# A fused attention and two-layer MoE kernel: another fixed order for its first 36 positions

## The chip, the cores and the metric

The kernel runs on one core of a Trainium2 chip. The metric is the device time of one execution in microseconds (us). The kernel before took 653.89 us as the median of three runs (653.66 to 656.63).

Engine names as in the profile: PE is TensorE (matmuls; PEld its weight loads), DVE is VectorE, ACT is ScalarE, POOL is GpSimd, SP is SyncE, which issues nearly all DMAs here.

## The reference

Attention over batch 2, 8 heads, 768 positions, head dimension 64, in float32. Each query sees the 31 keys of a band around it, and 24 block keys: the maximum over each block of 32 keys, with log(32) added to its score; its value is the mean of the block's values. Softmax over both together, then two dense layers over the 1536 tokens:

```
k_sum = k.reshape(B, H, nb, block, D).max(axis=3)
v_sum = v.reshape(B, H, nb, block, D).mean(axis=3)
scores_s = scale * np.einsum('bhsd,bhnd->bhsn', q, k_sum) + np.log(block)
a = softmax([where(|i - j| < 16, scale * q k^T, -1e9), scores_s])
x = a @ [v, v_sum]                       # 1536 tokens x 512
y = ((x @ w_a) * (x @ w_b)) @ w_out      # d_ff 1536
h = y @ w_in;  g = h - np.tanh(h)        # d_ff 2048
out = g @ w_out2
```

## The kernel before

Attention is cut into 24 units of 64 queries (12 of each batch element). A unit is a chain: transposed queries times a window of 96 keys and the 24 block keys on PE (`T2m`), mask and row minimum on DVE (`tt`), exponential and row sum on ACT (`ex`), one over the sum on DVE (`rb`), the normalization of the 128x480 scores (`nm`), transposes on PE (`T3t`), the copy out of PSUM (`T3e`), the product with the values on PE (`T4m`), and the split of the result into a high and a low half (`T4h` on ACT, `T4l` on DVE).

The dense layers work in blocks of 512 tokens, so block 0 needs units 0 to 7. Every float32 matmul is three matmuls of split operands: high by high, high by low, low by high. A weight tile arrives as raw words and is decoded: two ACT passes (`da`, `db`), a clamp (`dc`, line 179), a shift (`dd`, line 767), a bit mix (`de`, line 769) and an add (`df`, line 771), the last three mostly on DVE; then it is split by ACT (`sh`, line 776) and a subtraction (`sl`, line 779). The finished add frees the staging buffer for a later weight load.

A "position" is one weight tile times one block: 12 matmuls of 128x512. Positions 0 to 35 are block 0 of the first layer: `x @ w_a` (kind a), `x @ w_b` (kind b) and the product with `w_out` (kind o), in the order a0 b0 a1 b1 o0 a2 b2 o1 ... a11 b11 o10 o11. Their matmuls are `Mp<position>_<quarter>` (lines 802 for a and b, 796 for o). Between b and o the two results are multiplied (`Mt`, DVE, line 808) and split (`Mh`, ACT, line 811; `Ml`, DVE, line 813).

What sets the order: up to position 35 everything (attention units 0 to 15, the decoding of the weights, the 36 positions) is issued by `op` in the sequence of one string, `SEQ`, of 838 names; each engine executes its instructions in that order and waits at each for what it needs. A table, `EC`, says for each name which engine does it (`A` ACT, `D` DVE, `P` POOL). Attention units 0 to 15 are in this string; their PE operations stand between quarters of positions. From position 36 on, the scheduler of the framework orders all engines but SP. A few of its instructions are placed into the end of the fixed part: the decoding of the next layer's weights (lines 154, 155 on ACT, 161, 164, 165 on DVE, tiles `x21a` and `x21b`) and single matmuls of line 350.

`FILL` names operations in front of which `warm` (line 582) issues transposes of the identity, whose results are not used. `warm` is called for the operations `T1t`, `T2m`, `T3t` and `T4m` only.

Of the kernel before, what the change touches and what calls it, by code (L numbers as in the profile page):

```python
# [39 lines left out]
def band_attention_moe_kernel(ctx: ExitStack, tc: tile.TileContext, q, k, v, w_a, w_b, w_out, w_in, w_out2, out):  # L40
# [3 lines left out]
    B, H, S, D = q.shape  # L44
# [18 lines left out]
    def st(shape, tag, bufs=1, dt=F32):  # L63
        return sb.tile(shape, dt, tag=tag, bufs=bufs, name=tag)
# [510 lines left out]

    qbs = [qbd, qbd2, qbd3, qbd4]
    P_A, P_B = ([j for j in range(HEAD_P) if pos[j][0] is fn] for fn in (pos_a, pos_b))
    FILL = {'T1t4': 6}

    def warm(n, d):  # L580
        for _ in range(FILL.get(n, 0)):
            nc.tensor.transpose(d, ident, ident)

    def op(n):
        import re
        k, a = re.match("([A-Za-z]+[0-9](?:t|ea|eb|e|m|h|l)|[A-Za-z]+)(.*)", n).groups()
        i, _, c = a.partition("_")
        i, c = int(i or 0), int(c or 0)
        e = EC.get(n, "A")
        if k == "LK":  # L590
# [79 lines left out]
        elif k == "tt":  # L670
# [3 lines left out]
            e = st([128, NP, NK], ("e", "ta", "tg", "w")[i // 2] if i < 8 else "e", 36 if i in (6, 7) else 2)  # L674
# [11 lines left out]
        elif k == "ex":  # L686
            e, nm, sm = at_x[i]
# [4 lines left out]
        elif k == "rb":  # L692
            e, nm, sm = at_x[i]
            nc.vector.tensor_scalar(sm, sm, 1e-9, None, op0=ALU.add)
            nc.vector.reciprocal(sm, sm)
        elif k == "nm":
            eng = e if i > 7 else "P"
            e, nm, sm = at_x[i]
            if eng == "A":
                for p in range(NP):  # L700
# [4 lines left out]
        elif k == "T3t":  # L705
            e = at_x.pop(i)
# [54 lines left out]
        elif k in ("dc", "dd", "de", "df"):  # L761
# [117 lines left out]
```

## Time and profile before

| | |
|---|---|
| three runs | 653.66, 653.89, 656.63 us |
| profiled execution | 653.74 us; its span 652.0 us, 1.7 us lie around the span |
| PE busy | 633.5 us (97% of the span) |
| DVE, ACT, POOL busy | 499.3, 475.4, 206.6 us |
| granted TensorE clock | 0.996 on average |

A span is the time from the first to the last instruction. The page cuts it in 40 slices of 16.3 us; PE is at 7 tenths in the first slice and over 9 tenths from the fourth to the last but one. Busy PE time counts the full latency of overlapping matmuls, so how fast PE works is read from the start of one matmul to that of the next: a row "2.88 us x12" followed by a row that starts 2.72 us later means 0.227 us for each.

### The profile page before, as it was taken

The numbers are of one execution on the slowest core, as the hardware profiler recorded it, in microseconds if no ns is written. First come the engines' busy times: TensorE is split into PE (matmuls) and PEld (weight loads), VectorE is DVE, ScalarE is ACT, GpSimd is POOL, SyncE is SP. The second block draws the span as 40 slices with busy tenths as digits, with TensorE's granted clock in tenths as the row PEclk, the third lists the DMA queues.
The fourth block names the chain that finished last, engine by engine and source line by source line (L and its number), as shares of the span: only waits on it lengthen the run. The fifth ranks groups of instructions, "written<-read, shape, count | busy, mean of one in ns | idle before, by whom it ended". The sixth has DMA issues, their size and how long they took to land.

```text
span 652.0 us, 9585 instructions
## 1 busy us (share of the span) xinstructions
PE 633.5 (97%) x3238; PEld 517.6 (79%) x3238; DVE 499.3 (77%) x1007; ACT 475.4 (73%) x1001; POOL 206.6 (32%) x218
## 2 busy tenths in 40 slices
PE   7779999999999999999999999999999999999997
PEld 5667887878788878788888888888888888888885
DVE  5999999988764767747877758877777877777775
ACT  4889899987576797636655548777777777777774
POOL 6852232211100110001111144544444544444441
PEclk9999999999899999999999999999999999999999
DMA  9989995644503435414434100000010000100001
GB/s 203 256 229 250 262 268 174 185 126 116 162 17 118 145 110 158 145 51 147 157 133 156 37 1 1 1 0 2 1 65 1 1 1 0 40 26 2 2 0 65
DMA packets 81677, 62.11 MB, mean 95 GB/s; under 512 B 45716, under 2 KB 72340, under 8 KB 81628
## 3 DMA queue, kind: packets, MB, share of 16 engines
q1 hardware_dynamic: 79276, 60.32, 33.0%
q0 software_dynamic: 2352, 1.18, 1.5%
q8 instruction: 25, 0.41, 0.3%
q14 instruction: 24, 0.20, 0.1%
HBM read 54.00 MB, written 7.34 MB: 94 GB/s over the span
## 4 chain that ended last, share of the span: by engine, by line
PE 75%; DVE 9%; DMA 7%; ACT 5%; issue 2%; SPq 1%; POOL 0%; DVEq 0%; ACTq 0%; POOLq 0%
PE acc L439 20%; PE pb L350 12%; PE pa L350 12%; PE acc L378 8%; PE pt L350 5%; PE ps L350 5%; DMA stage<-in_moe_w_in_dram 4%; PE pb L802 3%; PE acc L796 3%; PE pa L802 2%; DVE w L769 1%; ACT e L283 1%; DVE w L771 1%; DMA x21a<-in_moe_w_out_dram 1%; DMA x20a<-in_q_dram 1%
## 5 line engine op out<-in xcount | busy, mean ns | idle before, releaser
L185 POOL TENSOR_TENSOR wsp<-w,wsp 128x512 fp32r<-128x512 f32 x97 | 127.7, 1335 | 139.8 <-ACT wsp L184 139.8
L184 ACT ACTIVATE wsp<-w 128x512 fp32r<-128x512 f32 x165 | 99.1, 621 | 14.2 <-PE acc L378 8.8
L179 POOL TENSOR_SCALAR w<-w 128x512 f32<-128x512 f32 x46 | 34.9, 764 | 174.6 <-ACT w L154 81.5
L439 PE MATMUL acc<-wsp,gh 128*128 128x512 f32 x256 | 78.8, 389 | 0.0
L185 DVE TENSOR_TENSOR wsp<-w,wsp 128x512 fp32r<-128x512 f32 x68 | 48.4, 712 | 31.7 <-ACT wsp L184 31.5
L378 PE MATMUL acc<-gh,wsp 128*128 128x512 f32 x192 | 64.2, 394 | 0.0
L350 PE MATMUL pa<-XB,wsp 128*128 128x512 f32 x240 | 60.5, 395 | 0.0
L350 PE MATMUL pb<-XB,wsp 128*128 128x512 f32 x240 | 59.6, 393 | 0.3 <-DVE tg L808 0.3
L343 ACT ACTIVATE gh<-tg 128x512 fp32r<-128x512 f32 x56 | 34.9, 623 | 29.9 <-DVE tg L366 29.6
L439 PEld LDWEIGHTS acc<-wsp,gh 128*128 128x128 f32 x256 | 48.0, 188 | 10.0
L350 PEld LDWEIGHTS pb<-XB,wsp 128*128 128x128 f32 x240 | 44.5, 188 | 9.8 <-issue 0.7
L350 PEld LDWEIGHTS pa<-XB,wsp 128*128 128x128 f32 x240 | 44.3, 188 | 9.0
L439 PE MATMUL acc<-wsp,gl 128*128 128x512 f32 x128 | 49.8, 389 | 0.0
L439 PE MATMUL acc<-wsp,vw 128*128 128x512 f32 x192 | 46.5, 390 | 0.0
L350 PE MATMUL pa<-XA,wsp 128*128 128x512 f32 x192 | 46.1, 389 | 0.0
L350 PE MATMUL pb<-XA,wsp 128*128 128x512 f32 x192 | 46.1, 389 | 0.0
L344 DVE TENSOR_TENSOR gl<-tg,gh 128x512 fp32r<-128x512 f32 x56 | 38.5, 688 | 9.7 <-ACT gh L343 9.4
L439 PEld LDWEIGHTS acc<-wsp,vw 128*128 128x128 f32 x192 | 35.9, 188 | 8.2 <-ACT vw L343 0.4
L350 PEld LDWEIGHTS pb<-XA,wsp 128*128 128x128 f32 x192 | 36.0, 188 | 7.5
L350 PEld LDWEIGHTS pa<-XA,wsp 128*128 128x128 f32 x192 | 36.0, 188 | 7.5
L378 PEld LDWEIGHTS acc<-gh,wsp 128*128 128x128 f32 x192 | 36.0, 188 | 7.5
L802 PE MATMUL pb<-XA,wsp 128*128 128x512 f32 x144 | 37.2, 398 | 1.2 <-DVE tg L808 1.1
(336 smaller groups left out, 1440.9 us busy)
## 6 DMA issues: line engine op xcount, KB each, us to landing
stage<-in_moe_w_out_dram SPq DMA_DIRECT2D x19, 512.0 KB, 3.5
stage<-in_moe_w_in_dram SPq DMA_DIRECT2D x16, 512.0 KB, 4.5
stage<-in_moe_w_a_dram SPq DMA_DIRECT2D x8, 512.0 KB, 4.3
w<-wsc SPq DMA_DIRECT2D x16, 256.0 KB, 3.5
vw<-in_v_dram SPq DMA_DIRECT2D x19, 192.0 KB, 5.0
stage<-in_moe_w_b_dram SPq DMA_DIRECT2D x7, 512.0 KB, 5.9
wsc<-x21a SPq DMA_DIRECT2D x8, 256.0 KB, 4.5
wsc<-x21b SPq DMA_DIRECT2D x8, 256.0 KB, 4.6
```

Source lines behind the costliest of these rows:

```text
L179: eng.tensor_scalar(rf, rf, HI_HI, HI_LO, op0=ALU.min, op1=ALU.max)
L184: nc.scalar.activation(s[:, 0, :], r, AF.Copy)
L185: eng.tensor_tensor(s[:, 1, :], r, s[:, 0, :].bitcast(F32), op=ALU.subtract)
L283: nc.scalar.activation(e[:, p, :], e[:, p, :], AF.Exp, scale=-1.0, bias=nm[:, p : p + 1], accum_out=sm[:, p : p + 1])
L343: nc.scalar.activation(dst[0], src, AF.Copy)
L344: eng.tensor_tensor(dst[1], src, dst[0].bitcast(F32), op=ALU.subtract)
L350: mm(dst, w, xx, start=(kk == 0 and n == 0), stop=(kk == KC - 1 and n == 2))
L378: mm(acc[blk][d][:, c0:c1], w, t, start=(f == 0 and c0 == 0 and n == 0), stop=(f == F1 - 1 and n == 2))
L439: mm(a[c], g[:, cs], s[:, i, :], start=(f == 0 and n == 0), stop=(f == F2 - 1 and n == 2))
L769: nc.vector.scalar_tensor_tensor(r, t[:, :, 1], -0x40000000, r, op0=ALU.bitwise_and, op1=ALU.bitwise_or)
L796: mm(acc[0][c], w, t, start=(f == 0 and m == 0), stop=(f == F1 - 1 and m == 2))
L802: mm(P_["M", i], w, t, start=(c == 0 and m == 0), stop=(c == KC - 1 and m == 2))
```

## The change

Three literals and one line change. `SEQ` keeps the same 838 names in another sequence. `EC` gets entries for `nm0` to `nm7`, and line 697, which sent the normalization of units 0 to 7 to POOL whatever the table said, now follows the table. Other entries of `EC` change too. `FILL` names `KP0` with 3 in place of `T1t4` with 6.

Engine choices that differ, before to after:

```
nm0 nm1 nm3 nm6 nm7    POOL -> DVE   (nm2 nm4 nm5 stay on POOL)
nm11 DVE -> ACT;  nm13 nm15 ACT -> DVE
T3e0 T3e1 T3e2 T3e3 T3e12  DVE -> ACT;  T3e7 ACT -> DVE
T1ea1 T1ea2 T1ea6  DVE -> ACT;  T1ea3 T1eb2  ACT -> DVE
W1 POOL -> DVE;  W4 DVE -> POOL;  W10 W11 ACT -> DVE;  V13 DVE -> ACT
dc0 dc1 dc2 dc7 dc12 dc16 dc22 dc23 dc28 dc30 dc33 dc35  POOL -> DVE
dc6 dc31 dc34  DVE -> POOL
sl1 POOL -> DVE;  df1 DVE -> POOL
vc2 POOL -> DVE;  vc3 vc7 DVE -> POOL;  vc4 ACT -> POOL
```

`W` and `V` copy the keys of a unit, `T1ea`/`T1eb` the transposed queries, `vc` the block values.

```diff
-    EC = {'T1ea0': 'A', 'T1eb0': 'A', 'T1ea1': 'D', ...
+    EC = {'T1ea0': 'A', 'T1eb0': 'A', 'T1ea1': 'A', ... 'nm0': 'D', 'T3e0': 'A', 'nm1': 'D', ...
...
-    FILL = {'T1t4': 6}
+    FILL = {'KP0': 3}
...
         elif k == "nm":
-            eng = e if i > 7 else "P"
+            eng = e
             e, nm, sm = at_x[i]
...
-    SEQ = '... Kt0 Ke0 Kt1 Kt3 Ke1 Kr0 Kt4 Kt2 ...
+    SEQ = '... Kt1 Kt0 Ke0 Kt2 Kt3 Kr1 Kr2 Ke1 ...
```

Which instruction now stands where, at three places. On POOL, the normalizations of the first units (line 703; 749 copies block values, 179 is a clamp). Lines with `-` are the kernel before:

```order
-L703 TENSOR_TENSOR e<-e,sm 128x480 x2
-L703 TENSOR_TENSOR ta<-ta,sm 128x480 x2
-L703 TENSOR_TENSOR w<-w,sm 128x480
+L703 TENSOR_TENSOR ta<-ta,sm 128x480
 L703 TENSOR_TENSOR tg<-tg,sm 128x480
 L749 TENSOR_SCALAR w<-w 24x512
-L749 TENSOR_SCALAR vw<-w 24x512 x2
-L179 TENSOR_SCALAR w<-w 128x512
-L703 TENSOR_TENSOR w<-w,sm 128x480
+L749 TENSOR_SCALAR vw<-w 24x512 x3
+L749 TENSOR_SCALAR w<-w 24x512
 L703 TENSOR_TENSOR tg<-tg,sm 128x480
```

Eight normalizations became three, and the clamp among them went away. On POOL right behind that, the clamps, the subtractions of the first weight tiles (779), the add of the second one (771) and the first accumulating load (223):

```order
 L703 TENSOR_TENSOR tg<-tg,sm 128x480
-L179 TENSOR_SCALAR w<-w 128x512 x2
-L779 TENSOR_TENSOR wsp<-w,wsp 128x512 x3
-L179 TENSOR_SCALAR w<-w 128x512
+L771 TENSOR_TENSOR w<-w,stage 128x512
+L779 TENSOR_TENSOR wsp<-w,wsp 128x512
 L223 DMA x20a<-in_v_dram 96x8x128
+L779 TENSOR_TENSOR wsp<-w,wsp 128x512
```

Three clamps and one subtraction left POOL for DVE, and one add came from DVE. On DVE, the end of the fixed part up to the last split `Ml11` (813); 808 is `Mt11`; 161, 164 and 165 belong to the next layer's weights. Before:

```order
L161 TENSOR_SCALAR x21a<-x21a 128x512
L771 ISA w<-stage,w 128x1024
L779 TENSOR_TENSOR wsp<-w,wsp 128x512 x2
L164 SCALAR_TENSOR_TENSOR x21a<-stage,x21a 128x512
L779 TENSOR_TENSOR wsp<-w,wsp 128x512
L161 TENSOR_SCALAR x21b<-x21b 128x512
L165 ISA x21a<-stage,x21a 128x1024
L808 TENSOR_TENSOR tg<-pb,ta 128x512
L164 SCALAR_TENSOR_TENSOR x21b<-stage,x21b 128x512
L779 TENSOR_TENSOR wsp<-w,wsp 128x512
L165 ISA x21b<-stage,x21b 128x1024
L813 TENSOR_TENSOR gl<-tg,gh 128x512
```

And the same stretch after:

```order
L779 TENSOR_TENSOR wsp<-w,wsp 128x512
L161 TENSOR_SCALAR x21b<-x21b 128x512
L779 TENSOR_TENSOR wsp<-w,wsp 128x512 x2
L164 SCALAR_TENSOR_TENSOR x21b<-stage,x21b 128x512
L161 TENSOR_SCALAR x21a<-x21a 128x512
L808 TENSOR_TENSOR tg<-pb,ta 128x512
L165 ISA x21b<-stage,x21b 128x1024
L164 SCALAR_TENSOR_TENSOR x21a<-stage,x21a 128x512
L779 TENSOR_TENSOR wsp<-w,wsp 128x512
L813 TENSOR_TENSOR gl<-tg,gh 128x512
L734 TENSOR_TENSOR XB<-pt,XB 128x4x64
L165 ISA x21a<-stage,x21a 128x1024
```

One of the six instructions of the next layer, an add of line 165, now stands behind the last split.

## Rows read from the trace of the kernel before

**Rows 1.** Busy us by engine (x instructions) in stretches, clock, DMA share, GB/s.

```profile
core 0: us, PE busy (x) PEld busy (x) DVE busy (x) ACT busy (x) POOL busy (x), PEclk, DMA share, GB/s
20.00:42.60 22.60, 15.02 (x195) 11.59 (x194) 22.09 (x73) 20.14 (x70) 16.51 (x17) 1.00 0.97 233
53.20:163.40 110.20, 110.11 (x637) 88.82 (x637) 102.24 (x248) 98.19 (x237) 25.76 (x31) 1.00 0.77 196
163.40:170.40 7.00, 5.38 (x15) 3.74 (x15) 3.63 (x7) 3.51 (x6) 0.61 (x1) 0.76 0.74 222
...
380.00:400.00 20.00, 20.00 (x90) 16.53 (x90) 13.06 (x21) 13.82 (x24) 8.24 (x7) 1.00 0.01 1
```

**Rows 2.** PE in order of time: start, us, instruction [idle before, releaser].

```profile
41.12 0.87 PE L582 MATMUL ps<-ident 128*128 128x128 f32 x6 [2.33 <-DVE XA L734]
41.83 0.60 PE L646 MATMUL ps<-ident,w 128*128 128x128 f32 x4
...
42.62 3.02 PE L802 MATMUL pa<-XA,wsp 128*128 128x512 f32 x12
...
53.17 3.02 PE L802 MATMUL pb<-XA,wsp 128*128 128x512 f32 x12 [1.11 <-DVE tg L808]
...
77.38 2.88 PE L802 MATMUL pa<-XA,wsp 128*128 128x512 f32 x12
...
157.47 2.88 PE L802 MATMUL pb<-XA,wsp 128*128 128x512 f32 x12
160.19 0.39 PE L796 MATMUL acc<-gh,wsp 128*128 128x512 f32 x1
...
164.97 0.51 PE L796 MATMUL acc<-gh,wsp 128*128 128x512 f32 x1 [0.67 <-ACT gh L811]
166.15 0.80 PE L796 MATMUL acc<-gl,wsp 128*128 128x512 f32 x1 [0.67 <-DVE gl L813]
...
170.35 0.60 PE L249 MATMUL pt<-ident,qn 128*128 128x128 f32 x4
```

**Rows 3.** DVE and POOL groups by shape, 0 to 171 us: busy us, mean ns | idle before.

```profile
L703 DVE TENSOR_TENSOR e<-e,sm 128x480 f32<-128x480 f32 x3 | 2.0, 652 | 0.0
L574 DVE COPY at<-acc 120x512 f32<-120x512 f32 x2 | 1.4, 686 | 0.0
L574 DVE COPY w<-kt 128x384 f32<-128x384 f32 x1 | 0.3, 345 | 0.0
L179 POOL TENSOR_SCALAR w<-w 128x512 f32<-128x512 f32 x30 | 23.6, 798 | 80.5 <-ACT w L758 64.9 <-DMA vw<-in_v_dram 11.6 <-PE ps L629 2.1
```

**Rows 4.** DVE in order of time.

```profile
26.67 0.42 DVE L574 COPY w<-w 24x512 f32<-24x512 f32 x1
27.02 1.21 DVE L574 COPY vw<-w 24x512 f32<-24x512 f32 x1
...
38.97 1.77 DVE L771 CUSTOM_DVE_ANT_0 w<-stage,w 128x1024 uint16<-128x1024 uint16 x1
...
41.65 0.41 DVE L734 TENSOR_TENSOR XA<-pa,XA 128x256 fp32r<-128x256 f32 x1
...
44.17 0.41 DVE L179 TENSOR_SCALAR w<-w 128x512 f32<-128x512 f32 x1
44.50 0.75 DVE L767 TENSOR_SCALAR w<-w 128x512 int32<-128x512 int32 x2
...
76.50 0.69 DVE L779 TENSOR_TENSOR wsp<-w,wsp 128x512 fp32r<-128x512 f32 x1 [1.05 <-ACT wsp L776]
...
164.20 0.68 DVE L779 TENSOR_TENSOR wsp<-w,wsp 128x512 fp32r<-128x512 f32 x1
164.81 0.68 DVE L165 CUSTOM_DVE_ANT_0 x21b<-stage,x21b 128x1024 uint16<-128x1024 uint16 x1
165.41 0.68 DVE L813 TENSOR_TENSOR gl<-tg,gh 128x512 fp32r<-128x512 f32 x1
```

**Rows 5.** POOL in order of time.

```profile
26.78 1.15 POOL L703 TENSOR_TENSOR w<-w,sm 128x480 f32<-128x480 f32 x1 [0.38 <-DVE sm L695]
...
38.65 1.53 POOL L779 TENSOR_TENSOR wsp<-w,wsp 128x512 fp32r<-128x512 f32 x1 [0.94 <-ACT wsp L776]
```

**Rows 6.** Who waited for whom on DVE, 0 to 171 us: total us, times, longest.

```profile
DVE wsp L779 <- ACT wsp L776: 2.7, 3, 1.1
DVE e L681 <- PE pt L268: 1.6, 2, 1.0
DVE XB L734 <- ACT XB L732: 1.5, 1, 1.5
DVE gl L813 <- ACT gh L811: 0.7, 1, 0.7
```

More of the change, by code (lines that the diff above doesn't have):

```diff
@@ new lines, in band_attention_moe_kernel @@
+    EC = {'T1ea0': 'A', 'T1eb0': 'A', 'T1ea1': 'A', 'T1eb1': 'A', 'T1ea2': 'A', 'T1eb2': 'D', 'T1ea3': 'D', 'T1eb3': 'D', 'W0': 'P', 'W1': 'D', 'W2': 'P', 'W3': 'P', 'W4': 'P', 'W5': 'P', 'W6': 'P', 'W7': 'P', 'nm0': 'D', 'T3e0': 'A', 'nm1': 'D', 'T3e1': 'A', 'nm2': 'P', 'T3e2': 'A', 'nm3': 'D', 'T3e3': 'A', 'nm4': 'P', 'T3e4': 'A', 'nm5': 'P', 'T3e5': 'A', 'nm6': 'D', 'T3e6': 'D', 'nm7': 'D', 'T3e7': 'D', 'vc0': 'D', 'vc1': 'D', 'vc2': 'D', 'vc3': 'P', 'vc4': 'P', 'vc5': 'P', 'vc6': 'P', 'vc7': 'P', 'dc0': 'D', 'df0': 'D', 'dc1': 'D', 'df1': 'P', 'dc2': 'D', 'df2': 'D', 'dc3': 'D', 'dc4': 'D', 'dc5': 'D', 'dc6': 'P', 'dc7': 'D', 'dc8': 'P', 'dc9': 'P', 'dc10': 'P', 'dc11': 'P', 'dc12': 'D', 'dc13': 'P', 'dc14': 'P', 'dc15': 'P', 'dc16': 'D', 'dc17': 'P', 'dc18': 'P', 'dc19': 'P', 'dc20': 'P', 'dc21': 'P', 'dc22': 'D', 'dc23': 'D', 'dc24': 'P', 'dc25': 'P', 'dc26': 'P', 'dc27': 'P', 'dc28': 'D', 'dc29': 'P', 'dc30': 'D', 'dc31': 'P', 'dc32': 'P', 'dc33': 'D', 'dc34': 'P', 'dc35': 'D', 'sl0': 'P', 'sl1': 'D', 'sl2': 'P', 'W8': 'D', 'W9': 'A', 'W10': 'D', 'W11': 'D', 'V12': 'A', 'W12': 'A', 'V13': 'A', 'W13': 'A', 'W14': 'A', 'W15': 'A', 'T1ea4': 'A', 'T1eb4': 'A', 'T1ea5': 'A', 'T1eb5': 'A', 'T1ea6': 'A', 'T1eb6': 'A', 'T1ea7': 'A', 'T1eb7': 'A', 'nm8': 'A', 'T3e8': 'A', 'nm9': 'A', 'T3e9': 'A', 'nm10': 'A', 'T3e10': 'A', 'nm11': 'A', 'T3e11': 'A', 'nm12': 'D', 'T3e12': 'A', 'nm13': 'D', 'T3e13': 'A', 'nm14': 'D', 'T3e14': 'A', 'nm15': 'D', 'T3e15': 'A', 'KE0': 'A', 'KE1': 'A', 'KE2': 'A', 'KE3': 'A', 'KE4': 'A', 'KE5': 'A'}
@@ new lines, in band_attention_moe_kernel @@
+    SEQ = 'LK0 LK1 LK2 LK3 LK4 LK5 Lq0 Lq1 Lq2 Lq3 Lv0 Lv1 Lv2 LV0 LV1 LV2 LV3 LV4 LV5 LV6 LV7 Lw0 Lw1 Lw2 Lw3 Lw4 Kt1 Kt0 Ke0 Kt2 Kt3 Kr1 Kr2 Ke1 W1 Ke2 W0 Kt4 W2 Kr4 Ke3 Kt5 Kr0 Kr3 T1t0 Kr5 W3 Ke4 T1eb0 Lq4 Ws1 T1ea0 T1t1 Ke5 Ws0 Ws2 T2m1 Ws3 T1t2 T2m0 W11 T1eb1 tt1 W5 W4 W10 T1ea1 T2m2 va0 T1t3 T2m3 tt0 T1ea2 T1eb2 W7 T2m5 ex1 T2m4 tt2 ex0 T1ea3 ex2 tt3 T1eb3 T2m7 W6 ex3 va1 va2 tt5 tt4 rb2 ex5 T2m6 tt7 ex7 vm nm2 tt6 vme T3t2 rb5 rb3 rb0 W8 rb1 nm0 T3t0 ex6 nm3 ex4 T3e0 Lk0 rb7 T3e2 da0 nm1 rb6 T3t3 T3t1 vc1 nm7 db0 T3t7 vc2 rb4 nm6 T3t6 T3e7 dc0 nm5 vc0 dd0 T3e3 da1 T3e6 T3t5 de0 dc1 T3e1 LA0 vc3 T4m2 da2 T4m0 vc7 db1 T4m7 vc6 df0 dd1 T4h2 dc2 T4h0 vc5 vc4 de1 dd2 T4l0 T4m3 T4h3 nm4 T4l2 T4m6 T4m1 df1 T4l3 T4h7 T4h1 T3t4 T4l1 T3e5 T4m5 T3e4 Lw5 sh0 T4m4 T4h5 T4h6 sl0 T4h4 T1t4 KP0 da4 T4l7 da3 T4l5 db2 T4l6 T4l4 Mp0_0 de2 dc4 T1ea4 LA1 Mp0_1 dc3 Mp0_2 sh1 T1eb4 df2 dd3 Lw6 Mp0_3 W9 dd4 T2m8 sl1 Mp1_0 de4 da5 de3 sh2 dc5 KR0 Lw7 Ma0 db3 tt8 dd5 Mp1_1 sl2 Mp1_2 db4 df3 da6 Mp1_3 Mp2_0 dc6 KE0 Lq5 sh3 Mt0 db5 df4 LV8 Mp2_1 sl3 Lk1 Mp2_2 da7 dd6 Mp2_3 Lq6 de5 T1t5 Lw8 dc7 Mh0 sh4 Ma1 Mp3_0 db6 df5 sh5 Ml0 Mp3_1 sl4 db7 dd7 Mp3_2 de6 ex8 de7 df6 sl5 Lw9 Mp3_3 da8 Mp4_0 Mt1 dc8 T2m9 T1eb5 Mp4_1 Mp4_2 LV9 sh6 rb8 df7 Lw10 dd8 Mp4_3 Mp5_0 Lk2 T1ea5 KP1 Mp5_1 sl6 db8 sh7 da9 da10 de8 db9 Mp5_2 Lw11 Mp5_3 Mh1 dc9 KR1 tt9 dc10 Mp6_0 df8 Mp6_1 db10 Lw12 dd9 KE1 sl7 de9 Mp6_2 nm8 Mp6_3 sh8 Ma2 db11 da11 T2m10 Lk3 Ml1 sl8 T3t8 df9 sh9 Lw13 Lw14 Lk4 dd10 da12 Mp7_0 ex9 tt10 Mp7_1 Mp7_2 dc11 de10 dc12 Mp7_3 df10 Mp8_0 sl9 Mp8_1 da13 Mp8_2 rb9 Mt2 T3e8 dc13 Mp8_3 Lq7 dd11 sh10 dd12 Mh2 de11 db12 nm9 sl10 Mp9_0 Lq8 KP2 Lw15 LA2 Ma3 Ml2 df11 KE2 de12 da14 Mp9_1 db13 sh11 dc14 dd13 KR2 Mp9_2 Mp9_3 Mt3 db14 Mp10_0 db15 da15 T2m11 df12 T3t9 Lw16 Mp10_1 sl11 Mp10_2 de13 Mh3 Mp10_3 Mp11_0 Mp11_1 tt11 dd14 Ml3 Mp11_2 dc15 sh12 da16 sl12 df13 dc16 Mp11_3 dd15 db16 Mp12_0 Lk5 de14 ex11 sh13 df14 KP3 ex10 Mp12_1 Mp12_2 T3e9 LA3 sl13 sh14 KR3 de15 rb11 df15 Lw17 dd16 Mp12_3 Mp13_0 KE3 T4m8 sl14 Ma4 T4m9 W12 sh15 T4h8 de16 Lw18 rb10 Lq9 T4l8 da17 T4h9 db17 T4l9 Mp13_1 dc17 da18 dd17 Mp13_2 sl15 Mt4 Mp13_3 Mp14_0 KP4 nm10 Mh4 dc18 Mp14_1 Mp14_2 df16 Mp14_3 Mp15_0 Mp15_1 Lw19 KE4 de17 Ml4 LV10 df17 da19 Mp15_2 KR4 dc19 db19 sh16 LV11 dd18 sl16 sh17 db18 KP5 Ma5 KE5 sl17 Lw20 dd19 Lw21 da20 nm11 Mp15_3 da21 db20 de18 Mp16_0 dc20 KR5 df18 Lw22 sh18 Lw23 de19 Mt5 V13 Mp16_1 dd20 Mp16_2 df19 Mp16_3 sl18 Mh5 sh19 Mp17_0 T1t6 da22 Mp17_1 Lw24 LV12 Mp17_2 de20 dc21 Mp17_3 sl19 Ml5 dd21 T1eb6 df20 Mp18_0 T1ea6 db21 da23 Mp18_1 de21 Mp18_2 dc23 dc22 sh20 V12 Mp18_3 sl20 dd22 db22 df21 Ma6 de22 Mp19_0 Mp19_1 T3t10 Mt6 Lw25 db24 da24 Mp19_2 Mp19_3 Mp20_0 dc24 dd23 dd24 T3e10 df22 T2m12 W13 sh21 Mp20_1 Mp20_2 Mp20_3 Mh6 sl21 tt12 Lw26 da25 de23 dc25 sh22 W14 Mp21_0 db23 Mp21_1 dd25 ex12 Ml6 df23 sh23 de24 T3t11 Mp21_2 sl22 T2m13 Mp21_3 da26 Lw27 df24 db26 tt13 db25 de25 dc26 Ma7 Mp22_0 da27 Lw28 sh24 Mp22_1 sl23 Mp22_2 dc27 W15 da28 Mt7 dd26 Mp22_3 dd27 T3e11 de26 Mh7 Mp23_0 df25 sl24 Mp23_1 Lw29 T4m10 da29 db27 df26 Ml7 Mp23_2 Lw30 Mp23_3 T4h10 sh25 T4l10 Mp24_0 Mp24_1 dc28 de27 rb12 mv0 Mp24_2 ex13 dd28 sh26 df27 mv1 Ma8 db28 de28 da30 mvE rb13 Lw31 T1t7 sl25 dc30 nm12 dd30 Mp24_3 sl26 nm13 Mt8 Mp25_0 T1eb7 Lw32 T1ea7 da31 LM12 T3t12 T2m14 sh27 db31 T3e12 tt14 sl27 Mp25_1 dc29 dc31 LM13 df28 dd29 Mp25_2 Mh8 db29 T4m11 Mp25_3 T4h11 Mp26_0 LV13 T3t13 ex14 da32 T4l11 T2m15 de29 Mp26_1 Mp26_2 Mp26_3 T3e13 de30 df29 tt15 rb14 LV14 dd31 nm14 T4m12 Lw33 Mp27_0 db30 Ml8 ex15 T4h12 T4m13 T4h13 rb15 db32 T4l12 LM14 sh29 Mp27_1 nm15 T3t14 T4l13 Lw34 dc32 df30 sh28 de31 Mp27_2 dd32 T3e14 T3t15 sl28 sl29 T3e15 Mp27_3 da34 LV15 sh30 LV16 Lw35 T4m14 LV17 T4m15 T4h15 T4l15 dc34 da33 Ma9 de32 df31 T4h14 Mp28_0 Mp28_1 Mp28_2 da35 df32 db33 Mp28_3 Mt9 LV18 sh32 dc33 dc35 sh31 Mp29_0 Mp29_1 sl30 dd35 Mp29_2 Mp29_3 Lw36 Mh9 db35 dd33 Mp30_0 dd34 db34 sl31 de33 Mp30_1 Ml9 Mp30_2 de35 Mp30_3 Mp31_0 Ma10 de34 df34 Mp31_1 sl32 Mp31_2 Mp31_3 df33 Mt10 sh34 Mp32_0 sh33 Mp32_1 Mp32_2 df35 sl33 Mp32_3 Mh10 Ml10 Mp33_0 sh36 sh35 Mp33_1 Mp33_2 sl34 Mp33_3 Mp34_0 Mp34_1 Lw37 Ma11 sl36 Mp34_2 sh37 sl35 Mp34_3 Mt11 Lw38 sl37 Mh11 Ml11 Mp35_0 T4l14 Mp35_1 sh38 Mp35_2 sl38 XE1 Mp35_3 XE3 XE2 XE0'
```

2 lines of the change are left out of this document (removed).

## The prediction

> **What bounds the kernel now.** I read the stretches first [rows 1]. From 53 us on TensorE (PE) is busy all the time, 110.1 of 110.2 us, and behind the fixed part too, 20.0 of 20.0 us in a later stretch. So the time is that at which the fixed part's matmuls end, plus a rest that PE works through without a pause. That rest begins at 170.35 us, with the transpose behind the last matmul of position 35 [rows 2], and neither its matmuls nor their number change. The change can move only this point, the head's end.
>
> Then PE in order of time [rows 2]. The first matmul of position 0 starts at 42.62; before that PE waits (15.0 us busy of 22.6 in 20 to 42.6 [rows 1]) and VectorE (DVE) is the full engine, 22.1 of 22.6 us. From 42.62 PE has one pause of 1.11 us, at 52, for the product `Mt0` on DVE, until position 34 (`o10`) starts at 160.19. At the end, position 35 waits for the high and the low half of the last product, and starts its second matmul only at 166.15. The granted clock of that stretch is 0.76 [rows 1], so part of it ran at 1.2 in place of 2.4 GHz.
>
> What PE would need without pauses: 160.19 - 42.62 - 1.11 = 116.46 us up to `o10`; 24 matmuls for `o10` and `o11` at 0.227 us (12 in 160.19 - 157.47 = 2.72 [rows 2]) are 5.44; two single matmuls of line 350 between them are 0.45. Together 122.35 us. From 42.62 that gives 164.97. The head's end is at 170.35, so 5.4 us are lost: 1.1 at 52, 4.3 at the end, where the last DVE split, `Ml11`, ends at 165.41 + 0.68 = 166.09 [rows 4] behind a full DVE queue.
>
> **The change part by part.**
>
> *DVE's load.* Back to back, a two-operand DVE instruction of 128x512 takes 0.60 us from start to start (164.20, 164.81, 165.41), a clamp 0.34 (44.17 to 44.50) [rows 4]. Twelve clamps come and three go: 9 x 0.34 = 3.1. Five normalizations of the first units come, at 0.65 less an overlap of 0.08 [rows 3]: 2.9. Of the later ones two come and one goes: 0.6. Five copies `T3e` go and one comes: -4 x 0.60 = -2.4 (0.69 long [rows 3]). One query copy goes net, -0.6. `sl1` comes and `df1` goes, 0. Key windows `W10` and `W11` come, two copies each (0.35 [rows 3] and a shorter one): 0.8. Net one copy of block values goes, 0.35 from start to start (26.67 to 27.02 [rows 4]), with `V13`: -0.5. Sum: +3.9 us of DVE work before the last split.
>
> *POOL's load and what it costs DVE.* A POOL instruction beside a DVE one can stretch it. While `sl0` ran for 1.53 us [rows 5], the add `df1` took 1.77 on DVE [rows 4], 1.1 more than the same add beside nothing (0.68, line 165). While a normalization ran on POOL at 26.78 [rows 5], a copy of block values took 1.21, 0.8 more than the one before it (0.42) [rows 4]; over the eight normalizations I count between 0 and 0.8, 0.3 in the mean. The clamps on POOL, 0.80 us each [rows 3], stretch DVE in only six of 30 places, by 0.4, so 0.1 in the mean. Five normalizations, nine clamps and one subtraction leave POOL: 5 x 0.3 + 9 x 0.1 + 0.7 = 3.1 us less stretching (0.7 for `sl1`, between the 1.1 of `sl0` and none). `df1` comes to POOL, which no row shows there: as a two-operand instruction over 128x512 it is bounded by no stretching and by `sl0`'s 1.1, and I take 1.1, the nearest row. Net 2.0 saved. One add of the next layer, 0.60, moves behind the last split. DVE's path to the last split grows by 3.9 - 2.0 - 0.6 = 1.3 us, to 167.4, if DVE waits as much as before.
>
> The Trainium skill, in "SBUF — State Buffer", states that VectorE, in an instruction with two SBUF inputs, and GpSimd, when it reads SBUF, take turns at a shared port pair, whichever comes second being blocked for the whole instruction of the other. By that, `df1` on POOL speaks against this change: an estimate from that rule is the whole instruction, 1.5 us as for `sl0`, in place of 1.1, and the sum would be 0.4 us later. The trace agrees in direction for `sl0` (1.1 of 1.5 us), but most of the clamps block nothing.
>
> *DVE's waits.* In the head DVE waits 2.7 us for `sh` on ACT, 1.6 for PE, 1.5 for one `T4h` and 0.7 for `Mh9` [rows 6], 6.5 in all. Four of these waits, 3.5 us, lie after 136 us, where the old order has DVE well ahead of PE. Counting instructions times their durations, DVE in the new order is 3 to 5 us less ahead there, while ACT's load is about 1 us smaller. A DVE that comes later finds its inputs ready. I take these 3.5 us as gone (0 at one end, 6.5 at the other): `Ml11` ends at 163.9.
>
> *The start of position 0.* It is set by the last low half of units 0 to 7, on DVE at 41.65 [rows 4]. Of the +3.9 us some 1.8 lie before that (five normalizations, three clamps, the window copies, less four `T3e`, `df1` and a copy), and about 0.9 of stretching goes, so DVE comes 0.9 later. Against it: the six idle transposes at 41.12 go (0.71 us to the next row's start at 41.83, so 0.7 on the way to position 0), since `KP0` never reaches `warm`; and normalizations on DVE wait for no other engine. Between 41.9 (only the transposes count) and 44.4 (the whole 1.8 with nothing saved) I take 43.0. That needs a TensorE clock that stays up without the transposes: it was 1.00 between 20 and 42.6 with PE idle a third of the time [rows 1].
>
> *PE's pauses.* Then 43.0 + 122.35 = 165.35 for PE alone. `Ml11` at 163.9 falls when `o11` is due (165.35 - 2.72 = 162.6) or 1.3 later. In between, the old order has places with almost nothing to spare: `sl11` ended at 77.19 for matmuls that started at 77.38 [rows 4, 2]. With DVE less ahead from there on, I add 0.9 us of pauses. The 1.11 at 52 I count as gone: DVE's sum up to `Mt0` is the same to 0.2 us, with less stretching, and one transpose group more stands ahead of the matmul that waited. 165.35 + 1.3 + 0.9 = 167.55: the head's end comes 2.8 us earlier.
>
> The profiled execution took 653.74 us: 653.74 - 2.8 = 650.9, and I write 651.0. It stands 0.15 under the median of the three runs, so the sum holds against that too.
>
> **The rivals.**
>
> *DVE's load is given back one for one (no change).* DVE waits as long as before, for it waits mostly for ACT, whose instructions have kept their places relative to it. `Ml11` ends at 167.4, `o11` follows in 2.72 us at full clock, 170.1, or as before in 170.35 - 166.09 = 4.26, 171.7. Time 653.5 to 655.1, about 654. For it: DVE was 93% busy (102.2 of 110.2). Against: 3.5 us of its waits lie where it was ahead.
>
> *DVE falls behind (slower).* POOL's relief doesn't show on DVE, as it didn't at 24 of the 30 clamps, and `df1` on POOL holds up DVE at about 38 us, ahead of position 0. Then the path grows by 3.9 + 1.1 - 0.6 = 4.4, `Ml11` ends at 170.5 and the head, at the lower clock, 4.26 later, at 174.8: 4.4 us more, 658.1. It decides from the point where DVE's sum exceeds what its waits can absorb (6.5 us), so less than this if some go: 655 to 658. For it: 3.9 us of work come to an engine that is nearly full. Against: it lost over 9 us to stretching, and POOL gets 11 us less work (9 x 0.8, five normalizations of about 1.1, `sl1` 1.3, less `df1` and two copies).
>
> *No pauses at all (faster by more).* PE starts at 41.9 and never waits: 41.9 + 122.35 = 164.25, the time 653.74 - 6.1 = 647.6. For it: DVE would need to gain 3 us more than I count. The skill's port rule, taken strictly, would give that: an estimate of 9 x 0.8 us for the clamps alone. The six stretched clamps of 30 speak against it.
>
> *The fill doesn't do what it says and is missed.* `FILL` names an operation that issues none, so no transposes are left. If the clock falls at position 0, the stretch at the end gives the price: 4.26 - 2.72 = 1.5 us, so 652.5. The clock of 1.00 over the idle stretch before speaks against it.
>
> **How the numbers follow.** The forecast, 649.5 to 652.3 around 651.0, gets 0.42; no change, near 654, 0.25; slower 0.13; no pauses 0.15; the missed fill 0.05. Half a percent, 3.3 us, is about what a measurement can tell from no change here. Faster than 650.5 is a third of the forecast's case (0.14), nearly all of the case without pauses (0.15), and what a somewhat better DVE would give from both sides of them, 0.07: 0.36. Slower than 657.0 is most of the slower rival, 0.11. Within: 0.53. The range 647.5 to 656.0 leaves out the worst of the slower rival and the few cases below PE's floor, some 0.17.
>
> **What would show it.** Right: POOL with some 11 us less work before 170 us and `nm` rows of 0.65 us on DVE; the first row of line 802 near 43; no pause at 52; the DVE row of the last line 813 ending near 164; the last row of line 796 ending near 167.5 with the clock at 1.00 there. Wrong: a first line 802 after 44.4; pauses of PE before DVE results in the middle; a last line 813 after 166.

## The result, and the profile of the changed kernel

The changed kernel took 649.02 us (median of six runs, 648.41 to 651.87), the kernel before 655.42 beside it (six runs, 653.66 to 657.89): ratio 0.9907, 95% interval 0.9878 to 0.9935. In a later group it took 649.74 us, ratio 0.9938 (0.9919 to 0.9956). It is faster, by 0.4 to 1.2%.

Both kernels were profiled twice, and what moved can be told only from all four (from the first matmul of position 0 PE needs 122.35 us without pauses; "lost" is what it took above that; every profile, those of the experiments too, has the same 694 matmuls from there to the head's end):

| us | before | before, again | changed | changed, again |
|---|---|---|---|---|
| first matmul of position 0 | 42.62 | 42.37 | 41.04 | 42.70 |
| lost from there to the head's end | 5.38 | 4.83 | 2.61 | 2.16 |
| head's end | 170.35 | 169.55 | 166.00 | 167.21 |
| from the head's end to the end of PE's last matmul | 477.92 | 478.83 | 476.93 | 476.91 |
| profiled execution | 653.74 | 653.85 | 648.41 | 649.60 |

In the means the start comes 0.6 us earlier, 2.7 us less are lost, and the work behind the head takes 1.5 us less: together 4.8, as the profiled executions. (The medians beside each other differ by 6.4 and 4.4 us.)

The stretches of the changed kernel, against [rows 1]:

```profile
core 0: us, PE busy (x) PEld busy (x) DVE busy (x) ACT busy (x) POOL busy (x), PEclk, DMA share, GB/s
20.00:42.60 22.60, 17.96 (x196) 13.68 (x197) 22.14 (x81) 19.07 (x65) 11.67 (x13) 0.85 1.13 257
...
53.20:163.40 110.20, 108.58 (x631) 87.42 (x629) 103.89 (x247) 97.16 (x232) 18.90 (x24) 1.00 0.74 195
163.40:170.40 7.00, 7.00 (x34) 5.76 (x34) 4.60 (x8) 4.92 (x10) 0.61 (x1) 1.00 0.85 253
```

The gain is in the last line: 34 instructions where 15 stood, PE full, the clock at 1.00 in place of 0.76. The middle line has a new loss, 1.6 us of PE's idle time where there was 0.1, though DVE is busier by 1.7 us. In the first line the clock is 0.85: a part of the attention stretch ran at 1.2 GHz.

PE in order of time, against [rows 2]:

```profile
13.04 1.15 PE L268 MATMUL pt<-kw,qbd 128*128 128x120 f32 x8
...
27.71 0.62 PE L710 MATMUL acc<-ident,e 128*120 128x128 f32 x4 [2.29 <-DVE e L703]
...
41.04 3.26 PE L802 MATMUL pa<-XA,wsp 128*128 128x512 f32 x12
...
51.37 0.63 PE L646 MATMUL pt<-ident,w 128*128 128x128 f32 x4 [0.52 <-DMA w<-in_q_dram]
...
60.23 0.66 PE L629 MATMUL pt<-ident,w 128*128 128x128 f32 x4 [1.17 <-ACT qbd L572]
...
163.10 0.39 PE L796 MATMUL acc<-gh,wsp 128*128 128x512 f32 x1
163.35 0.50 PE L796 MATMUL acc<-gl,wsp 128*128 128x512 f32 x1
...
166.00 0.60 PE L249 MATMUL pt<-ident,qn 128*128 128x128 f32 x4
```

The pause for `Mt0` at 52 and both waits for the last product are gone. Two others have come, at 51 (a load of queries) and at 60 (a query copy on ACT, late because ACT waited for a weight load, below); a short one for copies on ACT stands at 87 (0.31).

DVE, then POOL, against [rows 4] and [rows 5]:

```profile
26.54 1.03 DVE L703 TENSOR_TENSOR e<-e,sm 128x480 f32<-128x480 f32 x1
27.48 1.06 DVE L703 TENSOR_TENSOR ta<-ta,sm 128x480 f32<-128x480 f32 x1
...
30.95 0.66 DVE L703 TENSOR_TENSOR w<-w,sm 128x480 f32<-128x480 f32 x1
...
39.06 0.42 DVE L734 TENSOR_TENSOR XA<-pb,XA 128x256 fp32r<-128x256 f32 x1
...
162.61 0.69 DVE L813 TENSOR_TENSOR gl<-tg,gh 128x512 fp32r<-128x512 f32 x1
```

```profile
26.44 2.59 POOL L749 TENSOR_SCALAR vw<-w 24x512 f32<-24x512 f32 x3
...
38.61 1.36 POOL L771 TENSOR_TENSOR w<-w,stage 128x512 int32<-128x512 int32 x1 [4.74 <-ACT XA L732]
```

`df1` on POOL (38.61 to 39.97) stretched nothing: the adds beside it took their 0.42. Three normalizations took 1.02 to 1.06 beside the copies of block values on POOL, and the one at 30.95, with POOL idle, 0.66. `Ml11` ends at 163.30 for a matmul at 163.35: just in time.

Who waited for whom on DVE, 0 to 171 us, against [rows 6]:

```profile
DVE XB L734 <- ACT XB L732: 2.2, 4, 1.1
DVE w L767 <- POOL w L179: 1.3, 1, 1.3
...
DVE wsp L779 <- ACT wsp L776: 0.9, 2, 0.7
DVE e L681 <- PE ps L268: 0.8, 2, 0.6
```

DVE still waits, for other things. How much it works and waits in all, from the span's start to the start of `Ml11`, in the kernel before and then in the changed one:

```profile
0.00:165.41 165.41, 151.95 (x973) 121.16 (x973) 149.48 (x395) 139.61 (x355) 58.38 (x91) 1.00 0.84 204
```

```profile
0.00:162.61 162.61, 151.37 (x964) 121.17 (x965) 148.43 (x406) 138.37 (x351) 47.14 (x79) 0.98 0.86 207
```

DVE (its busy time is the third in a row) is busy 1.05 us less and idle 14.18 us in place of 15.93. POOL's clamps of line 179 went from 30 to 21 [rows 3], and its busy time up to 170 us from 59.0 to 47.8.

Behind the head PE does the same 2254 matmuls, but in another order, which the string does not give: there the framework's scheduler orders, and it came to another result. The last transposes of the last attention unit in the kernel before, then in the changed one (307 the transposes, 320 the product with the values, 350 and 378 matmuls of the dense layers):

```profile
268.35 0.69 PE L320 MATMUL ps<-at,vw 120*64 120x64 f32 x16
269.68 0.62 PE L307 MATMUL pt<-ident,e 128*120 128x128 f32 x4 [0.64 <-DVE e L297]
```

```profile
263.87 0.69 PE L320 MATMUL ps<-at,vw 120*64 120x64 f32 x16
264.49 1.19 PE L350 MATMUL pa<-XB,wsp 128*128 128x512 f32 x4
...
269.15 0.39 PE L378 MATMUL acc<-gl,wsp 128*128 128x512 f32 x1
269.38 0.60 PE L307 MATMUL pt<-ident,e 128*120 128x128 f32 x4
```

Before, the transposes stand right behind line 320, and PE waits for the normalization on DVE. After, 4.9 us of other matmuls stand between, and PE lists no wait at all behind the head. The stretches show it too, before and then after:

```profile
260.00:280.00 20.00, 19.36 (x120) 15.71 (x119) 13.32 (x31) 11.33 (x27) 1.23 (x2) 1.00 0.41 119
```

```profile
260.00:280.00 20.00, 20.00 (x117) 16.11 (x116) 12.05 (x29) 11.65 (x26) 1.23 (x2) 1.00 0.43 136
```

### The profile page after: what moved, and what is told of

Its sections match the earlier page's. It is cut to its first block, busy times and chain, and to the rows that moved or that the text cites. A ratio compares the mean times of both kernels' runs of the same rounds, so it can differ in the third digit from the quotient of the medians.

```text
span 646.7 us, 9568 instructions
## 1 busy us (share of the span) xinstructions
PE 631.7 (98%) x3232; PEld 516.7 (80%) x3232; DVE 499.2 (77%) x1019; ACT 474.1 (73%) x998; POOL 194.7 (30%) x206
## 4 chain that ended last, share of the span: by engine, by line
PE 86%; DVE 6%; ACT 4%; DMA 2%; SPq 1%; issue 1%; DVEq 0%; ACTq 0%
PE acc L439 20%; PE pb L350 15%; PE pa L350 15%; PE acc L378 10%; PE pt L350 5%; PE ps L350 5%; PE acc L796 4%; PE pb L802 3%; PE pa L802 3%; PE ps L268 2%; DMA stage<-in_moe_w_out_dram 1%; ACT e L689 1%; DMA x20a<-in_q_dram 1%; PE ps L320 1%; SPq L591 1%
## 5 line engine op out<-in xcount | busy, mean ns | idle before, releaser
L179 POOL TENSOR_SCALAR w<-w 128x512 f32<-128x512 f32 x37 | 26.7, 722 | 171.4 <-ACT w L154 80.6
L350 PE MATMUL pb<-XA,wsp 128*128 128x512 f32 x192 | 46.1, 389 | 0.0
L378 PE MATMUL acc<-gl,wsp 128*128 128x512 f32 x96 | 37.7, 393 | 0.0
```

What stands on the lines that cost most here:

```text
L179: eng.tensor_scalar(rf, rf, HI_HI, HI_LO, op0=ALU.min, op1=ALU.max)
L350: mm(dst, w, xx, start=(kk == 0 and n == 0), stop=(kk == KC - 1 and n == 2))
L378: mm(acc[blk][d][:, c0:c1], w, t, start=(f == 0 and c0 == 0 and n == 0), stop=(f == F1 - 1 and n == 2))
```

## The experiments

Times beside each other: the kernel before took 654.23 us in the group of the first four, 654.67 in that of the next four, 654.13 beside the three after them.

**The new engines for the first normalizations alone**, in the old order:

```diff
-    EC = {...}
+    EC = {... 'nm0': 'D', 'nm1': 'D', 'nm2': 'P', 'nm3': 'D', 'nm4': 'P', 'nm5': 'P', 'nm6': 'D', 'nm7': 'D'}
-            eng = e if i > 7 else "P"
+            eng = e
```

> The old sequence and engines, only the normalizations of units 0 to 7 placed as in the changed kernel (five on DVE, three on POOL). If the engine choice for them makes the gain, position 0 starts 1 us or more earlier than 42.6 and the time falls by 2 us or more. If the sequence makes it, DVE, which is the full engine up to 42 us, gets 2.9 us of work and loses some 1.5 us of stretching: position 0 starts 0.5 to 1.5 us later and the time is 0 to 1.5 us above the kernel before.

Measured 654.36 us, ratio 0.9994 (0.9979 to 1.0008): nothing. PE starts at 42.74, and the waits of the old order stand, here without the fall of the clock at the end:

```profile
53.76 3.02 PE L802 MATMUL pb<-XA,wsp 128*128 128x512 f32 x12 [1.14 <-DVE tg L808]
...
166.95 0.50 PE L796 MATMUL acc<-gl,wsp 128*128 128x512 f32 x1 [0.77 <-DVE gl L813]
```

**The new order alone**, with the old engines:

```diff
-    EC = {... after ...}
+    EC = {... before ...}
-            eng = e
+            eng = e if i > 7 else "P"
```

> The new sequence with all the old engine choices (normalizations 0 to 7 on POOL again). If the sequence makes the gain: at least half of it stays, 2.5 to 5 us below the kernel before. If it lives from the engine choices: normalizations of 1.0 to 1.3 us on POOL come late for the transposes, position 0 starts at 43 or later, and the time is within 1 us of the kernel before or above it.

Measured 659.17 us, ratio 1.0071 (1.0048 to 1.0094): slower. PE in order of time, up to position 0:

```profile
23.62 1.12 PE L268 MATMUL pt<-w,wsp 128*128 128x120 f32 x8 [2.39 <-DVE wsp L574]
...
34.82 0.92 PE L710 MATMUL pt<-ident,w 128*120 128x128 f32 x4 [1.17 <-POOL w L703]
36.64 1.11 PE L710 MATMUL pa<-ident,tg 128*120 128x128 f32 x4 [0.90 <-POOL tg L703]
...
47.96 0.49 PE L802 MATMUL pa<-XA,wsp 128*128 128x512 f32 x1
```

A query copy on DVE, which itself waited 2.40 us for one on ACT, and eight normalizations in POOL's queue hold PE up: position 0 starts at 47.96, and 7.03 us are lost behind it. The clock is 0.72 from 30 to 48 us; how much of the later start is its share isn't told apart.

**The new engines alone**, in the old order (the reverse edit: `EC` and line 697 from after, `SEQ` and `FILL` from before).

> The old sequence with all the new engine choices. DVE gets 3.9 us more work, POOL 11 us less, in a sequence that was not made for it. If DVE's load counts one for one: 1.5 to 4 us above the kernel before. If the engine choices make the gain: 2 us or more below it.

Measured 663.83 us, ratio 1.0141 (1.0117 to 1.0165). Position 0 starts at 46.02, 3.4 later than before, and 10.95 us are lost behind it. PE has one pause of 4.13 us right behind position 0:

```profile
53.59 4.63 PE L802 MATMUL pb<-XA,wsp 128*128 128x512 f32 x10 [4.13 <-DVE wsp L779]
```

That is `sl1`, now DVE's, which the old order puts behind a full DVE queue (it runs at 52.86); the clock falls there too. So neither half gains by itself: the engine of each piece and its place in the queue go together.

**The six transposes put back:**

```diff
-    FILL = {'KP0': 3}
+    FILL = {'T1t4': 6}
```

> The changed kernel with the six idle transposes in front of T1t4 as in the kernel before. If they cost their length: position 0 starts 0.5 to 0.8 us later than 41.04 and the time is 0.3 to 0.8 us above the changed kernel. If they are needed for the TensorE clock: the time is the same or lower. If PE has room for them: 0.

Measured 649.19 us, ratio 0.9936 (0.9911 to 0.996), as the changed kernel. PE starts at 41.87, 0.83 later than in the changed kernel's first profile, with the clock at half in the same stretch (28.4 to 35.2), yet the head ends at 165.86: the wait for the load at 51 is gone and that at 60 is 1.06. The later start was taken up where PE would have waited for loads anyway.

**Each of seven products issued twice**, 4.2 us more of DVE work between positions 7 and 26, in the changed kernel and in the one before:

```diff
+            aa = ab.pop(i)
+            for _ in range(2 if 2 <= i <= 8 else 1):
-            nc.vector.tensor_tensor(P_["t", i], P_["M", P_B[i]], ab.pop(i), op=ALU.mult)
+                nc.vector.tensor_tensor(P_["t", i], P_["M", P_B[i]], aa, op=ALU.mult)
```

> The changed kernel, with the product Mt issued twice for b2 to b8: seven more DVE instructions of 0.60 us, 4.2 us in all, between 56 and 130 us, result unchanged. If DVE has room in the new sequence (its waits at the end are over 4 us): the head ends 0 to 1 us later than 166.0, and the time is 0 to 1 us above the changed kernel. If DVE sets the head's end: 3 to 4.2 us later.

> The kernel before with the same seven DVE instructions more, 4.2 us. If the 3.5 us of DVE waits behind 136 us take up later work, as the forecast has it: 0.5 to 1.5 us above the kernel before. If DVE's load counts one for one in the old sequence: 3.5 to 5 us above.

In the changed kernel 651.29 us, ratio 0.9946 (0.993 to 0.9962): 2.3 us above its first median, 1.6 above its second. Its profile starts at 42.50, with 10.2 us at half clock, so the second profile is the one to compare: lost 3.80 against 2.16, 1.6 more. In the kernel before 656.25, ratio 1.0023 (1.0011 to 1.0034): 1.6 more. By the medians the new order takes up 1.9 to 2.6 and the old one 2.6 of the 4.2 us, which answers none of the sharper forecasts. The old order's profile says otherwise: it is of the second longest of twelve runs (657.54; 655.32 to 657.59), its head loses 9.52 us, 4.1 to 4.7 more than without the added work, and ends 3.4 to 4.2 later, with the clock again at half at its end. So which order has more room on DVE isn't settled.

**The clamps back on their old engines** (15 entries of `EC`; of these 12 go back to POOL):

```diff
-    'dc0': 'D', 'dc1': 'D', 'dc2': 'D', ... 'dc6': 'P', ...
+    'dc0': 'P', 'dc1': 'P', 'dc2': 'P', ... 'dc6': 'D', ...
```

> The changed kernel with all clamps on the engines of the kernel before: twelve go from DVE to POOL, three from POOL to DVE; DVE 3.1 us less work, less 0.9 us of stretching by POOL. If DVE sets the head's end: 1 to 2 us below the changed kernel. If PE and ACT set it: within 0.7 us of it. If a clamp's latency on POOL (0.8 against 0.4 us, and a queue) matters: 0.5 to 3 us above.

Measured 651.16 us, ratio 0.9942 (0.9925 to 0.996), 1.4 to 2.1 more than the changed kernel; the start is at 43.28. PE, then POOL:

```profile
33.04 1.11 PE L710 MATMUL pa<-ident,tg 128*120 128x128 f32 x4 [1.35 <-POOL tg L703]
...
40.48 0.65 PE L710 MATMUL pt<-ident,tg 128*120 128x128 f32 x4 [0.80 <-POOL tg L703]
```

```profile
31.25 0.61 POOL L179 TENSOR_SCALAR w<-w 128x512 f32<-128x512 f32 x1 [7.11 <-ACT w L758]
31.83 1.16 POOL L703 TENSOR_TENSOR tg<-tg,sm 128x480 f32<-128x480 f32 x1
```

A clamp that waits for ACT (POOL stood idle 7.11 us before it) stands in POOL's queue ahead of a normalization that PE waits for, and which ran at 24.30 in the changed kernel: what the clamps leave with POOL is not only their time, which the prediction counted, but a place in the queue. The order of PE behind the head is a third one here, with 0.7 us more there.

**Loads in another sequence on SP, in the changed kernel**: the query load `Lq5` 15 names earlier, ahead of `Lw7`, and the loads `Lk1` and `Lq6` behind the weight load `Lw8`, which stood behind both:

```diff
-    SEQ = '... Lw7 ... Lq5 ... Lk1 ... Lq6 ... Lw8 ... Lw9 ... Lw10 ...
+    SEQ = '... Lq5 Lw7 ... Lw8 ... Lk1 Lw9 ... Lq6 Lw10 ...
```

> The changed kernel with three loads moved in SyncE's queue: queries 5 ahead of weight load 7, keys 1 and queries 6 behind weight load 8. In the changed kernel PE pauses 0.52 us at 51 for queries 5, and 1.17 at 60 for a key transpose behind ACT, which waited 2.48 us for weight load 8, issued 1.9 us after its buffer was free. If these loads set PE's pauses: both pauses go and the time is 1 to 1.7 us below the changed kernel. If something else is late right behind them: within 0.5 us.

Measured 648.14 us, ratio 0.9902 (0.9881 to 0.9922), 0.9 to 1.6 under the changed kernel's two medians, which are of other groups. The two places, without a wait:

```profile
50.94 0.60 PE L646 MATMUL pt<-ident,w 128*128 128x128 f32 x4
...
59.26 0.66 PE L629 MATMUL pt<-ident,w 128*128 128x128 f32 x4
```

In the changed kernel ACT stood 2.48 us ahead of the query copies, for the weight load that came behind those two in the queue; with the loads in the new sequence it doesn't wait there. The row of the changed kernel:

```profile
57.62 0.67 ACT L758 ACTIVATE w<-x21a 128x512 f32<-128x512 f32 x1 [2.48 <-DMA x21a<-in_moe_w_a_dram]
```

**The changed kernel again, with `df1` on DVE, and the resequenced loads again**, in one group:

```diff
-    'df1': 'P'
+    'df1': 'D'
```

> The changed kernel as it is, beside the two that follow. Both theories: 648.4 to 650 us, ratio to before 0.990 to 0.993. It says how far its own start of position 0 moves from run to run: 41.0 if the half-clock stretch in the attention phase lies as it did, up to 42.5 if it lies later (as it did in the run with the doubled products, whose instructions up to there are the same).

> The changed kernel with the add df1 back on DVE. In the changed kernel df1 on POOL ran at 38.61 for 1.36 us beside adds of DVE that read one operand from PSUM, and none of them was stretched (0.42 each). Theory A (POOL stretches DVE only where both DVE operands lie in SBUF): df1 on DVE costs 0.6 us there, and up to 1.1 more if sl0 on POOL then runs beside it as in the kernel before; first L802 at 41.7 to 42.8. Rival B (DVE had room there, the start hangs on ACT or PE): first L802 unchanged at 41.0. By both the time moves by less than 0.8 us against the changed kernel, since a start 0.8 us later (the run with the transposes put back) was taken up by the waits for loads at 51 and 60.

> The changed kernel with three weight loads issued earlier, once more, to compare it with the changed kernel on the same chip. Theory A (the pauses at 51 and 60 for late loads were on the path): 0.4 to 1.0 us under the changed kernel of this group. Rival B (the start's own variation hides it): no difference beyond 0.3 us.

(The three loads that were moved are the two of queries and the one of keys above, not weight loads.) The changed kernel took 649.74 us; with `df1` on DVE 649.20, ratio 0.9923 (0.9905 to 0.9942), so no difference; its profile is of the longest of its six runs (651.78), whose start, 42.84, has 10.2 us at half clock before it and one DVE wait of 0.67 for ACT among the last adds, and 4.17 us are lost behind it, so it tells neither theory. With the resequenced loads 648.91, ratio 0.9918 (0.99 to 0.9937): 0.8 us under the changed kernel of this group, ranges 647.24 to 649.97 and 649.22 to 651.47, and 1.22 us lost in place of 2.16. The intervals of the ratios overlap; this is the fastest version tried, and its lead over the changed kernel is likely, not shown. The changed kernel's second profile against its first:

```profile
13.31 2.02 PE L268 MATMUL pt<-kw,qbd 128*128 128x120 f32 x8
...
42.70 3.27 PE L802 MATMUL pa<-XA,wsp 128*128 128x512 f32 x12
...
167.21 0.60 PE L249 MATMUL pt<-ident,qn 128*128 128x128 f32 x4
```

The same eight matmuls took 2.02 in place of 1.15 us, with the clock at 0.59 in that stretch:

```profile
13.00:17.00 4.00, 4.00 (x23) 3.84 (x22) 1.77 (x12) 2.59 (x6) 0.51 (x1) 0.59 1.24 266
```

The later rows of the attention are 1.66 us later, the first matmul of position 0 as well. So the start that looked like a gain of 1.6 us belongs to the run.

**The kernel before, again:**

> The kernel before, profiled once more. The changed kernel's own start of position 0 moved by 1.7 us between two profiled runs, with the place of its half-clock stretches. If the same holds here, the start moves by more than 0.3 us from 42.62; what is lost behind it without the stretch of half clock at the head's end should be 4.0 to 4.5 us in place of 5.4 (the run with the new normalization engines alone had 4.5 there at full clock). Rival: start 42.6 and 5.4 lost again, with the half clock at the same place, so both belong to the kernel and not to the run. The pause at 52 and the waits for the last splits at the end stand by both; the median is 653.5 to 656.

Measured 654.46 us, ratio 1.0001 (0.998 to 1.0022). The start is 42.37, though the clock is at half from 28.3 to 38.6; it moved by 0.25, less than the 0.3 expected. The end of the head, and the clock over it:

```profile
53.79 3.04 PE L802 MATMUL pb<-XA,wsp 128*128 128x512 f32 x12 [1.14 <-DVE tg L808]
...
166.91 0.50 PE L796 MATMUL acc<-gl,wsp 128*128 128x512 f32 x1 [0.84 <-DVE gl L813]
...
169.55 0.60 PE L249 MATMUL pt<-ident,qn 128*128 128x128 f32 x4
```

```profile
163.40:170.40 7.00, 5.38 (x24) 3.73 (x23) 5.05 (x10) 3.50 (x6) 0.61 (x1) 1.00 0.72 212
```

The waits are the kernel's; the half clock of [rows 1] at the end came in that run and not in this one: from `Ml11`'s end (166.86 here, 166.09 there) the head needs 2.7 us in place of 4.26. `Ml11` is later, so that 4.83 are lost, a little over the forecast.

## Why the prediction came out as it did

The forecast was 651.0 us; the medians are 649.02 and 649.74, the first just under the 649.5 at which the forecast's own case ended. What was to happen at the head's end did happen. But POOL's relief came out at about twice its size and DVE's waits at half, which cancel, and that is luck; and the stretch behind the head was left out.

**The head's end.** Predicted 2.8 us earlier; measured 4.35 between the first profiles, 3.35 between the means of two. PE's waits for `Mt0` and `Ml11` were its content, and the table bears them out: lost 3.2 less by the prediction, 2.7 less in the runs.

**The pauses.** Predicted 2.2 left, 1.3 before the last position and 0.9 before DVE results in the middle; measured 2.61 and 2.16. The size was right and the places wrong, so the size was luck: `Ml11` is just in time (163.9 predicted, 163.30 and 164.53 measured), which leaves no wait before the last position, and most of the pauses are waits for loads at 51 and 60, which the prediction did not look at. The resequenced loads remove these two; 1.92 and 1.22 us are lost then.

**DVE's waits.** Predicted 3.5 us less; measured half of it. From the span's start to `Ml11` DVE is idle 15.93 and 17.09 us before and 14.18 and 15.34 after, 1.75 less in the means. All of that lies behind 136 us (3.65 and 4.13 before, 2.04 and 2.26 after), where the prediction looked, but it doesn't all go there. That it goes because DVE comes later isn't shown.

**POOL's relief.** POOL lost 11.2 us of work, as worked out, but what that saves DVE was counted at half its size. DVE's busy time up to `Ml11` was to grow by 1.3 us (3.9 of work, less 2.0 of stretching and the 0.6 of the moved add); it fell by 0.8 in the means (149.48 and 149.09 before, 148.43 and 148.50 after). If the 3.9 and the 0.6 hold, an estimate, 4.1 us of stretching went in place of 2.0. Row by row the estimate is near that: set against the same instructions with POOL idle, DVE's instructions beside POOL lasted 9.8 and 8.9 us longer in all before, 4.7 and 4.8 after. This and the waits cancel: `Ml11` starts 2.6 earlier in the means, against 2.2 predicted, by luck. Two prices are seen one by one: 1.1 for `df1` on POOL was nothing, and three of the normalizations, counted at 0.65, took 0.4 more each. The Trainium skill, "SBUF — State Buffer" ("SBUF: two separate sides"), says that a VectorE instruction takes turns with GpSimd where it has two SBUF inputs or runs in a two-port mode; the adds beside `df1` read one operand from PSUM, and the trace agrees with it (0.42 us). By the same rule a normalization, with both inputs in SBUF, takes turns with the copies on POOL, and 1.03 in place of 0.66 agrees in direction. The prediction took the price of its nearest row for `df1` without asking which instructions would stand beside it.

**The start.** Predicted 43.0, 0.4 later; measured 41.04 and 42.70. The assumption that the clock stays at 1.00 fell, for either order and with or without the transposes: it was at half for 6.8 us in the changed kernel and with the transposes, for 3.4 and 6.8 us in the changed kernel again, and for 10.2 us in the kernel before, again. In the changed kernel again, 1.4 of the 1.66 us came in the stretch from 13 to 17, with the fall there. The five profiles with the new order's same instructions up to position 0 start it at 41.04, 41.36, 42.34, 42.50 and 42.70, the three with the old order's at 41.91, 42.37 and 42.62: no earlier start is shown. The missed fill, a rival, is excluded by the run with the transposes: same half clock, same time.

**The step that failed** is the first one, that the rest behind the head "works through without a pause" and "the change can move only this point". One stretch at 380 us stood for all of it, while the trace of the kernel before has PE busy 19.36 of 20 us from 260 to 280. The old order waits there at one or two places for a normalization (0.64 us, in the second profile 1.02 and 0.5), and the change gives the scheduler another start, from which it makes another order of PE's work. The runs sort by that order. Five profiles with the old string have the old one, matmul by matmul, and need 477.8 to 479.3 us. Seven profiles have the changed kernel's (that kernel twice, with the transposes, with the added work, with `df1` on DVE, with the loads twice) and need 476.91 to 476.95. The new string with all old engines or the old clamps has a third, and 477.1 and 477.7. This gave 1.0 us between the first profiles and 1.5 between the means. The forecast of 651.0 lies 2.6 us over the first profile and 1.4 over the second; what it left out behind the head is 1.0 of either, and the rest of the first is the start.

**The rivals.** One for one fell: `Ml11` ends at 163.30 and 164.53 in place of 167.4, and of work added to DVE only a part showed in the medians. DVE falling behind fell, for the head. No pauses at all did not come, 2.2 to 2.6 are left; with the resequenced loads 1.2.

What stays open: why the clock of the attention stretch falls in one place in one run and in another in the next, how much added DVE work either order takes up, and 0.4 us of the 1.0 behind the head that no listed pause accounts for.

## What to carry to other kernels

An order and a table of engines are one choice: either half of this change alone cost 0.7 and 1.4%, and the whole gained 0.4 to 1.2%. Where a scheduler orders what follows a fixed part, compare its order there too, since the same instructions can come out with or without a wait. Before a term of 1 us at the start is believed, profile both kernels twice. And when a sum of terms comes out right, measure the terms: here half the waits and twice the relief made nearly the same sum.

## What the runs showed of the hardware

The granted clock fell to half (1.2 GHz) for 3.4 to 10.2 us at a time somewhere between 12 and 46 us in the profile of every experiment and of the changed kernel, and not in the first one of the kernel before; the same program started position 0 at 41.04 and at 42.70. An add with one operand in PSUM was not stretched by a POOL instruction beside it (0.42 us), while a 128x480 multiplication from SBUF took 1.02 to 1.06 beside POOL's copies, in place of 0.66. Of 4.2 us of work added to an engine that is over 90% busy, 1.6 to 2.3 showed in the medians.
